# Two Fourier stages by sums and differences on quarter arrays, and operations recorded when they are counted ready

## The chip, the core and the metric

The kernel runs on one core of one Trainium2 chip. The metric is the device time of one execution in microseconds (us). TensorE (PE) multiplies matrices into PSUM, VectorE (DVE) and ScalarE (ACT) read and write PSUM and SBUF, GpSimd (POOL) works in SBUF and issues indirect DMAs, and SyncE (SP) issues the other DMAs. Each engine works through its own queue in order. PSUM is used as seven banks of 128x512 numbers and one more for logits.

## The reference

`x` has 8 batches of 2496 rows with 256 channels. Along the rows a filter is applied in the frequency domain, and every row of the result then goes through one of eight experts:

```python
X = np.fft.rfft(x, axis=1)
y = np.fft.irfft(X * (filt_r + 1j * filt_i), n=2496, axis=1)
x = y.reshape(19968, 256)
logits = x @ w_gate                          # 8 experts
expert_idx = np.argmax(logits, axis=1)
gate_w = softmax(logits)[row, expert_idx]
out[row] = gate_w * (np.maximum(x[row] @ w1[e], 0) @ w2[e])   # w1 256x1024, w2 1024x256
```

All numbers are float32.

## The kernel before

A Fourier transform of 2496 = 39 x 64 rows is done in two steps, of 39 points (index q) and of 64 points (index t). Each batch goes through four stages. `stage_a` (line 498) multiplies by the table `tas`, which has the cosines and sines of 39 points three times along its diagonal: 3 values of t lie in 3 x 39 = 117 partitions, and 3 x 40 rows come out, 20 cosine and 20 sine rows for each. 22 such columns of 256 channels make a batch, and they come in chunks of four, `CH`, the last of two. A matmul takes two columns, 512 numbers a partition. The result goes through the DRAM tensor `zd` to change its layout. `stage_b` (511) does the 64 points and multiplies by the filter, `stage_c` (533) goes back over 64 points and writes `ud`, and `stage_d` (548) goes back over the 39 points with the table `tds`. Batch 0 goes through SBUF instead of DRAM (`first_a`, `turn_z`, `first_c`, `turn_u`). From `stage_d`'s rows the logits are made (`turn_y` with `logits`, or from batch 3 on `block_logits`), `route` (707) finds each row's expert and its place in a sorted list, and `scatter` writes the rows to the DRAM tensor `rowsd` by an indirect DMA. `tile_map` plans expert tiles of 512 rows (256 and 128 at the start and the end).

The experts' work: `rows_in` loads a tile, `turn_x` (954) transposes it in blocks on DVE, `hidden_by_quarters` (979) forms the hidden layer by seven products of quarter matrices with sums of weights (`w1_sums`) and rows (`sums`) from POOL, and `result` (1042) multiplies by the second weights, scales by the gate and writes the output by an indirect DMA.

The order is worked out while the program is built. `Order` (125) wraps the engines: each call goes to the real engine at once and is counted with an estimated duration, so that it has a clock for every engine and a ready time for every tile. The main loop (from 1287) picks PE's next step: the steps of the Fourier stages stand in the list `STEPS` (made by `slot`, 1071, one slot for each batch), the products of the experts in two streams, and `share` decides how much of each. A step is taken when what it needs is counted ready. `either` (373) gives an evacuation of PSUM to DVE or to ACT, whichever is counted to end first. What a step makes other engines do is recorded at that place, and so stands in their queues in PE's order:

```python
def issue(*args, **named):
    self.order.count(self.name, op, args, named)
    return real(*args, **named)
```

`flush` and `more_loads` record the stores and loads on SP's queue, `prefetch` the loads of rows and weights, `side` a piece of `route`. All calls are recorded in the line 238, so the profile tells operations apart by their tiles: `fin` is a loaded chunk of any stage, `zo`, `uo` and `yo` are what stages one, three and four write, `hT` the hidden layer, `xg` and `xT` an expert tile's rows before and after transposition, `w1t` and `w2t` weights.

Of the kernel before, what the change touches and what calls it, by code (L numbers as in the profile page):

```python
# [34 lines left out]
TK = NB * NS  # L35
DH = D // P
# [4 lines left out]
NJ = D // CT  # L41

# [13 lines left out]
def dft_tables():  # L56
# [25 lines left out]
    ids = np.zeros((NB, N1, NG))  # L82
    valid = np.zeros((NB, N1, NG))
    for j in range(NB):
        for i in range(len(range(j, N2, NB))):
            ids[j, :, i] = token(q, NB * i + j)
            valid[j, :, i] = 1.0

    by_block = np.zeros((4, CT, NG + 2))
    by_block.reshape(P, NG + 2)[:TP, :NG] = valid.reshape(TP, NG)  # L90
# [5 lines left out]
        "ta": ta.reshape(TP, TK),  # L96
        "tb": tb,
        "tc": tc,
        "td": np.pad(td.reshape(TK, TP), ((0, 0), (0, P - TP))),
        "sg": np.concatenate([sg[:, :NF // 2], sg[:, NF // 2:]]),  # L100
        "ids": ids.reshape(TP, NG),
        "valid": np.concatenate([np.pad(valid.reshape(TP, NG), ((0, P - TP), (0, 0))), by_block], axis=1),
    }


def lay_x(x):

    out = np.zeros((x.shape[0], P, NG, D), x.dtype)
    q = np.arange(N1)
    for j in range(NB):  # L110
        for i in range(len(range(j, N2, NB))):
            out[:, j * N1:(j + 1) * N1, i] = x[:, token(q, NB * i + j)]
    return out
# [11 lines left out]
class Order:  # L125
# [3 lines left out]
    LOAD = 2.0  # L129

    def __init__(self, nc):
        self.nc = nc
        self.t = dict.fromkeys(("tensor", "vector", "scalar", "gpsimd", "sync", "transfers"), 0.0)
        self.slow = self.busy = self.last = 0.0
        self.done, self.used, self.slots, self.ahead = {}, {}, {}, {}
        self.tensor, self.vector, self.scalar, self.gpsimd, self.sync = (
            Issue(self, name) for name in ("tensor", "vector", "scalar", "gpsimd", "sync"))
# [6 lines left out]

    def ready(self, *aps):
        times = [a for a in aps if isinstance(a, float)]
        return max([0.0] + times + [self.done.get(key, 0.0) for a in aps if not isinstance(a, float) for key in self.parts(a)])
# [29 lines left out]
    def count(self, engine, op, args, named):  # L177
        aps = [a for a in list(args) + list(named.values()) if isinstance(a, bass.AP)]
        if not aps:
            return  # L180
# [6 lines left out]
        at = named.get("out_offset")  # L187
        if at is not None:
            ins.append(at.ap)
        kept = [a for a in ins if a.space != DRAM or a.name[:2] in ("zd", "ud")]  # L190
        free = self.t[engine]
        start = max([free] + [self.ready(a) + (self.HOP if engine != "sync" else 0.0) for a in kept])
        if out is not None:
            start = max(start, self.ahead.pop(out.name, 0.0))
            n = int(np.prod([d[1] for d in out.ap][1:])) if out.space != DRAM else 0
        tail = 0.0
        if op.endswith("dma_start"):
            busy = 1.3 if engine == "gpsimd" else 0.4
            self.t[engine] = start + busy
            took = self.transfer(out, named["in_"])  # L200
            self.t["transfers"] = max(self.t["transfers"], start + busy) + took
            end, tail = self.t["transfers"], self.LOAD
        else:
            if out is None:
                took = 0.02
            elif engine == "tensor":
                if start > self.busy + 1.2:
                    self.slow = start + 3.4
                rows = out.ap[0][1]
                took = max(0.1, 0.00085 * n) if op == "transpose" else max(0.216, 0.00169 * n) if rows > 32 else 0.00045 * n  # L210
                took *= 2.0 if start < self.slow else 1.0
                tail = 0.25
            elif engine == "vector":
                took = 0.15 + n / 960
            elif engine == "scalar":
                took = 0.16 + n / 1200
            else:
                took = 0.2 + n / 480
            end = self.t[engine] = start + took
            if engine == "tensor":  # L220
                self.busy = end
# [4 lines left out]
        self.last = end + tail  # L226


class Issue:
# [3 lines left out]
    def __getattr__(self, op):  # L233
        real = getattr(getattr(self.order.nc, self.name), op)

        def issue(*args, **named):
            self.order.count(self.name, op, args, named)
            return real(*args, **named)  # L238

        return issue  # L240


class Slots:
    def __init__(self, order, pool, bufs):
        self.order, self.pool, self.bufs, self.tiles, self.n = order, pool, bufs, {}, {}

    def free(self, tag, k=0):

        past, n = self.tiles.get(tag, []), self.n.get(tag, 0)
        if len(past) + k < n or k >= n:  # L250
            return 0.0
        name = past[k - n]
        return max(self.order.done.get(name, 0.0), self.order.used.get(name, 0.0)) + 0.1

    def tile(self, shape, dtype, **named):
        new = self.pool.tile(shape, dtype, **named)
        past = self.tiles.setdefault(named.get("tag") or named.get("name"), [])
        n = self.n[named.get("tag") or named.get("name")] = named.get("bufs") or self.bufs
        if len(past) >= n:
            name = past[-n]  # L260
            self.order.ahead[new.name] = max(self.order.done.get(name, 0.0), self.order.used.get(name, 0.0)) + 0.1
        past.append(new.name)
        return new


@with_exitstack
def kernel(
# [39 lines left out]
    TR = E * TE  # L307

# [16 lines left out]
    prow = perm.tile([P, 1], I32, name="prow")  # L325
    need = perm.tile([1, 1], I32, name="need")
    ps = open_pool(ctx, name="ps", bufs=7, space=PSUM)

# [4 lines left out]

    tas = cst.tile([TP, TK], F32, name="tas")
    tbs = cst.tile([P, P], F32, name="tbs")
    tcs = cst.tile([P, P], F32, name="tcs")
    tds = cst.tile([TK, P], F32, name="tds")
# [15 lines left out]
    ids0 = cst.tile([TP, NG], F32, name="ids0")  # L353
    vld = cst.tile([P, 2 * NG + 2], F32, name="vld")
# [8 lines left out]
    def experts_pool():  # L363
        first.close()
# [8 lines left out]
    def either(i, n, on_vector, on_scalar):  # L373

        ready = nc.ready(i)
        if max(t["vector"], ready) + 0.15 + n / 960 <= max(t["scalar"], ready) + 0.16 + n / 1200:
            on_vector()
        else:
            on_scalar()

    def evac(o, i, n):
        either(i, n, lambda: nc.vector.tensor_copy(o, i), lambda: nc.scalar.copy(out=o, in_=i))
# [8 lines left out]
    def load_filters(c):  # L391
        f0, n = FH[c]
        if c == 0:
            nc.sync.dma_start(out=tbs, in_=tb)
# [11 lines left out]
        if c == 0:  # L406
            nc.sync.dma_start(out=tcs, in_=tcm)

    def load_rest():
        nc.sync.dma_start(out=tds, in_=td)  # L410
# [33 lines left out]
    def columns(ap, i0, n):  # L444
# [3 lines left out]
        yield TK, slice(0, m), rows[i0 * TK:(i0 + m) * TK, :].rearrange("(i p) d -> p i d", p=TK)  # L448
        if m < n:
            yield NS, slice(m, n), rows[(NG - 1) * TK:, :].rearrange("(i p) d -> p i d", p=NS)  # L450

    ins, outs, lgs, yts, lands = {}, {}, {}, {}, []
    NIN, YB = 7, 6
# [17 lines left out]
    def by_part(ap):  # L471

        return ap.rearrange("t (c f) d -> (t c) f d", c=2)

# [8 lines left out]
    def load_z(b, c):  # L483
        f0, n = FH[c]
        zi = fin(("z", b, c))
        nc.sync.dma_start(out=zi[:, :n], in_=by_part(zd[b])[:, f0:f0 + n, :])

    def load_u(b, c):
        i0, n = CH[c]
        ui = fin(("u", b, c))  # L490
        for r, m, v in columns(ud[b], i0, n):
            if r == TK:

                v = bass.AP(v.tensor, v.offset, [[D, P]] + [list(k) for k in v.ap[1:]])
                r = P
            nc.sync.dma_start(out=ui[:r, m], in_=v)

    def stage_a(b, c):
        i0, n = CH[c]
        xt = ins.pop(("x", b, c))  # L500
        zo = sb.tile([TK, 4, D], F32, tag="st", name="zo", bufs=4)
        for j in range(0, n, 2):
            p = bank()
            mm(p[:TK, :], lhsT=tas, rhs=xt[:TP, j:j + 2, :], start=True, stop=True)
            evac(zo[:, j:j + 2, :], p[:TK, :].rearrange("p (t d) -> p t d", t=2), 512)
        for r, m, v in columns(zd[b], i0, n):
            move(v, zo[:r, m])
# [3 lines left out]
    def stage_b(b, f):  # L511
# [6 lines left out]
        mm(p, lhsT=tbs, rhs=zi[:, j:j + 2, :], start=True, stop=True)  # L518
# [9 lines left out]
        if b == 0 or b < 3 and not sides:  # L528
            nc.gpsimd.tensor_tensor(ys, ys, yw, op=ALU.add)
        else:  # L530
            nc.vector.tensor_tensor(ys, ys, yw, op=ALU.add)

    def stage_c(b, f):
# [6 lines left out]
        mm(p, lhsT=tcs, rhs=ys, start=True, stop=True)  # L540
        evac(uo[:, j:j + 2, :], p.rearrange("p (i d) -> p i d", i=2), 512)
        if j == 2:
            f0 = f - 2
            move(by_part(ud[b])[:, f0:f0 + 4, :], uo)
# [3 lines left out]
    def stage_d(b, c):  # L548
# [8 lines left out]
        for j in range(0, n, 2):  # L557
            p = bank()
            if i0 + j + 2 < NG:
                mm(p, lhsT=tds, rhs=ui[:TK, j:j + 2, :], start=True, stop=True)  # L560
            else:

                for i, k in enumerate((TK, NS)):
                    mm(p[:, i * D:(i + 1) * D], lhsT=tds[:k, :], rhs=ui[:k, j + i, :], start=True, stop=True)
            evac(yo[:, j:j + 2, :D], p.rearrange("p (i d) -> p i d", i=2), 512)

# [824 lines left out]
```

## Time and profile before

| | before |
|---|---|
| median of 3 runs (lowest, highest) | 1497.58 us (1494.55, 1498.59) |
| profiled execution | 1494.36 us |
| its span, first to last instruction | 1492.7 us |
| mean granted clock of PE in it | 0.991 |
| PE, DVE, ACT, POOL busy | 1451.7, 770.7, 471.8, 733.4 us |
| memory read and written | 196.45 and 80.64 MB |

In a group's line the names are what is written <- what is read, then partitions x numbers; of a matmul the rows*columns of the array in use come first. Behind x stands how many there were, then their busy time together, the mean duration of one, the engine's idle time before them, and what ended it. PEld is the loading of weights into the array, beside PE. A float32 product is two records of PE.

### The profile page before, as it was taken

The numbers are of one execution on the slowest core, as the hardware profiler recorded it, in microseconds if no ns is written. First come the engines' busy times: TensorE is split into PE (matmuls) and PEld (weight loads), VectorE is DVE, ScalarE is ACT, GpSimd is POOL, SyncE is SP. The second block draws the span as 40 slices with busy tenths as digits, with TensorE's granted clock in tenths as the row PEclk, the third lists the DMA queues.
The fourth block names the chain that finished last, engine by engine and source line by source line (L and its number), as shares of the span: only waits on it lengthen the run. The fifth ranks groups of instructions, "written<-read, shape, count | busy, mean of one in ns | idle before, by whom it ended". The sixth has DMA issues, their size and how long they took to land. (4 is left out here: it accounts for less than half of the span.)

```text
span 1492.7 us, 24448 instructions
## 1 busy us (share of the span) xinstructions
PE 1451.7 (97%) x7396; PEld 1148.8 (77%) x7396; DVE 770.7 (52%) x1732; ACT 471.8 (32%) x983; POOL 733.4 (49%) x1053
## 2 busy tenths in 40 slices
PE   8898997999989999999999999999999999999998
PEld 6553555776667777777787888887888889999997
DVE  4667677354577656565764555537344334441110
ACT  4453442333322233222233222222222222223332
POOL 3434455344446656554555756764546455741111
PEclk9999999999999999999999999999999999999999
DMA  9749889678767756474456545545455543456661
GB/s 255 252 152 333 289 306 295 207 258 280 251 182 229 219 157 169 131 239 128 128 152 196 130 117 149 147 139 145 151 178 176 167 146 106 117 187 179 181 179 52
DMA packets 216376, 278.10 MB, mean 186 GB/s; under 512 B 124131, under 2 KB 163708, under 8 KB 216245
## 3 DMA queue, kind: packets, MB, share of 16 engines
q1 hardware_dynamic: 197125, 233.19, 52.7%
q0 software_dynamic: 19120, 43.33, 8.3%
q8 instruction: 62, 1.02, 0.3%
q14 instruction: 69, 0.57, 0.1%
HBM read 196.45 MB, written 80.64 MB: 186 GB/s over the span
## 5 line engine op out<-in xcount | busy, mean ns | idle before, releaser
L238 DVE TENSOR_TENSOR hT<-bank,hT 128x512 f32<-128x512 f32 (+1 forms) x504 | 300.7, 627 | 298.9 <-PE bank L238 183.1
L238 PE MATMUL bank<-w2t,hT 128*128 128x256 f32 x1984 | 447.5, 382 | 1.0 <-DVE hT L238 0.5
L238 PEld LDWEIGHTS bank<-w2t,hT 128*128 128x128 f32 x1984 | 377.6, 191 | 62.9 <-issue 9.5
L238 POOL DMA_INDIRECT out_dram<-ys,ng x161 | 160.7, 998 | 459.7 <-ACT ys L238 183.3
L238 PE MATMUL bank<-xT,w1t 128*128 128x256 f32 (+1 forms) x1728 | 316.7, 329 | 0.3 <-DVE xT L238 0.3
L238 PEld LDWEIGHTS bank<-xT,w1t 128*128 128x128 f32 x1728 | 266.8, 192 | 36.5 <-issue 11.8
L238 ACT ACTIVATE hT<-hT 128x1024 f32<-128x1024 f32 (+1 forms) x144 | 133.9, 958 | 378.7 <-DVE hT L238 374.8
L238 POOL DMA_INDIRECT rows<-yo,row x176 | 180.3, 1025 | 69.0 <-POOL yo L238 36.0
L238 ACT ACTIVATE ys<-bank,ng 128x256 f32<-128x256 f32 x128 | 60.6, 473 | 369.6 <-PE bank L238 297.0
L238 PE MATMUL bank<-sums,wsum 128*128 128x256 f32 (+1 forms) x576 | 135.7, 358 | 2.8 <-DVE hT L238 1.8
L238 PE MATMUL bank<-w2s,hT 128*128 x592 | 132.6, 380 | 0.0
L238 PEld LDWEIGHTS bank<-w2s,hT 128*128 128x128 f32 x592 | 110.5, 191 | 13.6
L238 PEld LDWEIGHTS bank<-sums,wsum 128*128 128x128 f32 x576 | 101.2, 191 | 20.1 <-issue 7.3
L238 DVE TENSOR_TENSOR ys<-bank,ht 128x512 f32<-128x512 f32 x80 | 55.0, 688 | 81.9 <-PE bank L238 77.3
L238 PE MATMUL bank<-fin,tas 117*120 117x512 f32 x154 | 76.9, 620 | 11.9 <-DMA fin<-in_x_dram 11.9
L238 PE MATMUL bank<-fin,tds 120*128 120x512 f32 (+1 forms) x168 | 76.6, 576 | 6.0 <-DMA fin<-ud 6.0
L238 DVE STREAM_TRANSPOSE xT<-xg 128x512 f32<-128x512 f32 (+2 forms) x126 | 57.5, 494 | 44.2 <-PE bank L238 44.2
L238 PE MATMUL bank<-fin,tbs 128*128 128x512 f32 x140 | 72.6, 605 | 2.5 <-DMA fin<-zd 2.5
L238 ACT ACTIVATE hT<-bank 128x128 f32<-128x128 f32 (+1 forms) x192 | 58.1, 304 | 50.1 <-PE bank L238 42.4
L238 PE MATMUL bank<-ys,tcs 128*128 128x512 f32 x140 | 72.7, 604 | 1.0 <-DVE ys L238 1.0
L238 POOL TENSOR_TENSOR wsum<-w1t 128x256 f32<-128x256 f32 x72 | 53.4, 742 | 38.1 <-PE bank L238 36.5
L238 PE MATMUL bank<-xT,wsum 128*128 128x256 f32 (+1 forms) x288 | 68.3, 360 | 0.3 <-DVE hT L238 0.3
(150 smaller groups left out, 1491.5 us busy)
## 6 DMA issues: line engine op xcount, KB each, us to landing
w1t<-in_moe_w_dram SPq DMA_DIRECT2D x126, 512.0 KB
w2t<-in_moe_w_dram SPq DMA_DIRECT2D x68, 512.0 KB
fin<-in_x_dram SPq DMA_DIRECT2D x39, 512.0 KB
fin<-zd SPq DMA_DIRECT2D x35, 512.0 KB
ud<-uo SPq DMA_DIRECT2D x35, 512.0 KB
fin<-ud SPq DMA_DIRECT2D x35, 512.0 KB
zd<-zo SPq DMA_DIRECT2D x35, 480.0 KB
xg<-rows SPq DMA_DIRECT2D x112, 128.0 KB
```

The source lines that it names most:

```text
L238: return real(*args, **named)
```

## The change

Three things change together.

First, in batches 3 to 7 (`BQ = 3`) stages one and four use that the cosine of q and of 39 - q is the same and the sine the opposite. The rows are laid out so that q and 39 - q stand in the same partition, in columns two apart; `fold_x` replaces a loaded chunk by sum and difference, cosines are taken of the sums and sines of the differences, from 60 partitions each, and the four products of a chunk (cosine or sine, first or second 64 partitions) each use a quarter of the array. Stage four does the reverse, `fold_y` makes rows q and 39 - q from the two parts. Batches 0 to 2 keep their stage one; their stage four and their routing go by the new layout of rows, in which 124 partitions are used where there were 117 and unused places are sent to an index past the end of the list, which the scatter drops. Each table has a second version, loaded when the last batch of the first is through.

Second, calls to DVE, ACT and POOL are held (`Held`) and recorded when their start is counted to be no later than PE's clock, in the order of these starts; operations that can run on either of two engines choose only then. A matmul or DMA that needs a held one's result has it recorded first. PE's steps count a tile that a held operation writes as not ready.

Third, smaller edits: PSUM banks and load buffers are taken in the order in which they come free; `turn_x` transposes in place (`xg`, three buffers, read in runs of 32) where it wrote `xT`; the hidden layer is in halves, and `result` takes them in the order in which they are finished; weights and rows are asked for only when a buffer is counted free within 0.5 us; the addition at the end of `stage_b` is given to DVE or POOL by counted time; a tiny memset stands between two row scatters that follow each other on POOL.

```diff
 class Order:
+    def given(self, engine, op, args, named):
+        if self.caught is not None:
+            self.caught.append((engine, op, args, named))
+            return None
+        if engine in self.HELD and self.hold:
+            self.held.append(Held(self, [(engine, op, args, named)]))
+            return None
+        out, ins = self.operands(op, args, named)
+        self.clear([key for a in ins for key in self.parts(a)], self.parts(out) if out is not None else [])
...
+    def advance(self):
+        while True:
+            free = [(work.begin(), k) for k, work in enumerate(self.held) if not work.behind]
+            begin, k = min(free, default=(self.NEVER, 0))
+            if begin > self.t["tensor"]:
+                return
+            self.held[k].go()
...
+    def issue(self, engine, op, args, named):
+        if engine == "gpsimd":
+            row = op == "indirect_dma_start" and named["out"].name[:4] == "rows"
+            if row and self.rows_last:
+                self.nc.gpsimd.memset(self.between, 0.0)
...
+class Held:
+    def go(self):
+        while self.behind:
+            next(iter(sorted(self.behind, key=self.order.held.index))).go()
...
+        made = order.issue(*min(self.ways, key=end))
...
     def evac(o, i, n):
-        either(i, n, lambda: nc.vector.tensor_copy(o, i), lambda: nc.scalar.copy(out=o, in_=i))
+        nc.one_of(lambda: nc.vector.tensor_copy(o, i), lambda: nc.scalar.copy(out=o, in_=i))
...
-    NIN, YB = 7, 6
+    NIN, YB, OB = 7, 6, 1
...
+    def fold_x(b, c):
+        m = CH[c][1] // 2
+        xt = ins["x", b, c]
+        od = outs["od", b, c] = sb.tile([P, 2, D], F32, tag="od", name="od", bufs=OB)[:, :m]
+        sums(od, xt[:, :m], xt[:, m:2 * m], ALU.subtract)
+        sums(xt[:, :m], xt[:, :m], xt[:, m:2 * m], ALU.add)
...
     def stage_a(b, c):
-        for j in range(0, n, 2):
-            p = bank()
-            mm(p[:TK, :], lhsT=tas, rhs=xt[:TP, j:j + 2, :], start=True, stop=True)
-            evac(zo[:, j:j + 2, :], p[:TK, :].rearrange("p (t d) -> p t d", t=2), 512)
...
+            od = outs.pop(("od", b, c))
+            both = [bank()[:, :m * D].rearrange("p (t d) -> p t d", t=m) for _ in range(2)]
+            for c2, of in enumerate((xt, od)):
+                for h in range(2):
+                    k = slice(64 * h, 64 * h + TH)
+                    mm(both[h][64 * c2:64 * c2 + 64], lhsT=ta[k, 64 * c2:64 * c2 + 64], rhs=of[k, :m], start=True, stop=True)
+            for h in range(2):
+                evac(zo[:, h * m:(h + 1) * m, :], both[h], m * D)
...
     def stage_d(b, c):
+        for h in range(2):
+            last = i0 + n == NG and h == 1
+            for k in range(2):
+                if b < BQ:
+                    rows, cols = slice(0, NS if last else TK), slice(64 * k, 64 * k + 64)
+                else:
+                    rows, cols = slice(64 * k, 64 * k + (NF if last else TH)), slice(0, 64)
+                mm(both[k][64 * h:64 * h + 64], lhsT=tds[rows, cols], rhs=ui[rows, h * m:(h + 1) * m, :], start=True, stop=True)
...
+    def sums(o, i0, i1, op):
+        nc.one_of(*(lambda on=on: on.tensor_tensor(o, i0, i1, op=op) for on in (nc.vector, nc.gpsimd)))
+
+    def fold_y(b, c):
+        m = CH[c][1] // 2
+        yo, odd = outs["o", b, c], outs.pop(("odd", b, c))
+        sums(yo[:, m:2 * m, :D], yo[:, :m, :D], odd, ALU.subtract)
+        sums(yo[:, :m, :D], yo[:, :m, :D], odd, ALU.add)
...
     def turn_x(i):
-        xts[i] = pools["moe"].tile([P, DH, 4 * P], F32, tag="xT", name="xT", bufs=2)
-        for dh in range(DH):
-            nc.vector.transpose(xts[i][:, dh, :n * P].rearrange("p (g r) -> p g r", r=QW), xg[:, :n * NQ, dh, :])
+        xg = xg[:, :n * NQ]
+        nc.vector.transpose(xg, xg)
+        xts[i] = xg.rearrange("p g h r -> p h g r")
...
     def result(i, j):
-        for k in range(FT):
+        for m, k in enumerate((0, 1, 4, 5, 6, 7, 2, 3)):
...
     def slot(k):
+        for name, of, at, when in (("ta", ta, BQ - 1, "a"), ("tb", tb, BQ, "b"), ("tc", tcm, BQ, "c"), ("td", td, BQ + 1, "d")):
+            if k == at:
+                steps.append((-1.0, lambda name=name, of=of: load_table(name, of, 1), None, 0.0, when))
...
+                    steps.append((at - 0.04, lambda c=c: fold_x(k + 1, c), ("x", k + 1, c), 0.0, "x", lambda c=c: count("od") < OB and [ins["x", k + 1, c]]))
...
     def prefetch():
-        if i < min(len(work), NT - RARE) and rows_at[work[i][3]] <= t["tensor"] and i - used["x"] < 2:
+        if i < min(len(work), NT - RARE) and rows_at.get(work[i][3], nc.NEVER) <= t["tensor"] and i - used["x"] < 2 and i - halves[0] // 2 < 3 and soon("xg"):
...
             flush()
             more_loads()
+            nc.advance()
```

## The prediction

> **What bounds the kernel now.** I read the page from the top: busy time by engine first, then what TensorE (PE) waits for, then the timeline and the groups of the two stages that change.
>
> ```profile
> span 1492.7 us, 24448 instructions
> PE 1451.7 (97%) x7396; PEld 1148.8 (77%) x7396; DVE 770.7 (52%) x1732; ACT 471.8 (32%) x983; POOL 733.4 (49%) x1053
> PEclk9999999999999999999999999999999999999999
> DMA  9749889678767756474456545545455543456661
> ```
>
> PE is the bound: 41.0 us of the span without a matmul, and every other engine is idle for about half. DMA is near full only in the first quarter. So a matmul taken away shortens the span wherever PE has other products to go on with. The list of PE's waits says what the idle time is:
>
> ```profile
> PE bank L238 <- DMA fin<-in_x_dram: 12.3, 6, 6.9
> PE bank L238 <- DMA fin<-ud: 6.0, 1, 6.0
> PE bank L238 <- DVE hT L238: 3.6, 4, 1.8
> PE lt L238 <- DVE yt L238: 3.1, 1, 3.1
> PE bank L238 <- DMA fin<-zd: 2.5, 2, 2.3
> ```
>
> The columns are total, times, longest. Loads end 20.8 us (three lines), other engines some 14 us (two of these lines and eight smaller ones). All of it lies before 1050 us, nearly all before 450 us (the other 6 us of the 41 are the span's end). The groups, by form, give the stages that change:
>
> ```profile
> L238 PE MATMUL bank<-fin,tas 117*120 117x512 f32 x154 | 76.9, 620 | 11.9 <-DMA fin<-in_x_dram 11.9
> L238 PE MATMUL bank<-fin,tds 120*128 120x512 f32 x140 | 68.0, 610 | 6.0 <-DMA fin<-ud 6.0
> ```
>
> 154 records stand for the 77 products of batches 1 to 7 with 11 each, so a product is two passes. The 620 ns overlap the next pass; what one costs is the distance between starts, from the timeline:
>
> ```profile
> 637.24 1.88 PE L238 MATMUL bank<-fin,tbs 128*128 128x512 f32 x4
> 638.95 1.89 PE L238 MATMUL bank<-xT,w1t 128*128 128x256 f32 x8
> ...
> 303.67 2.11 PE L238 MATMUL bank<-w2t,hT 128*128 128x256 f32 x9
> 305.70 0.65 PE L238 MATMUL lt<-yt,wb 128*32 128x128 f32 x16
> 306.28 1.13 PE L238 MATMUL bank<-xT,w1t 128*128 128x256 f32 x4
> ```
>
> From 637.24 to 638.95 four passes of 512 columns take 1.71 us: 0.43 each (0.216 for 256 columns, by the eight passes to 640.68). The lower lines are the nearest to the new form: 16 passes of 128 columns, each in a strip of 32 columns of the array. One after the other they would take 16 x 0.11 = 1.76; they take 305.70 to 306.28, 0.58 us. So four strips run side by side, four rounds of 0.11. Changing to strips and back costs the rest: nine passes of 0.216 after 303.67 end at 305.61, 0.09 before the strips start, and 0.58 - 0.44 = 0.14 behind them: 0.23 us in and out.
>
> **The change part by part.**
>
> Stage one, batches 3 to 7. Before: 5 x 11 products of two passes at 0.43 = 47.2 us. After, by the order of the built program: 25 groups of four 64x64 products of 512 columns and 5 of 256. If all four run side by side a group is two passes, 0.86 or 0.43: 23.6. Gain 23.6.
>
> Stage four, batches 3 to 7. Before: 5 x 10 products at 0.86, and the last pair of columns in 5 x 4 passes of 256 at 0.27 to 0.31 (distance of starts), 1.16 a batch: 48.7. After: 25 x 0.86, and 5 x 0.86 for the last one, whose 60-row and 20-row parts follow each other: 25.7. Gain 23.0. Together 46.6.
>
> Changes of tiling. The order shows 263 changes of the array's form after, 127 before: 136 more, 68 in-and-out pairs at 0.23: +15.6. Strips of 32 columns are the nearest row; quarters of 64x64 have no row. Ends: 0.09 x 136 = 12.2, and twice the pair, 31.
>
> Stage four, batches 0 to 2, also changes: 120x64 products, the two of the lower output half before the two of the upper, on the same strip. Beside each other they cost what two full products did; if the second pair comes up only when the first pair's last pass starts, a group takes three rounds of two passes' time where two were: +0.86 on 15 groups, +13 at most. The trace shows one waiting pass being overtaken by other strips, not three; I take +5, ends 0 and +13. Nine mask multiplications more on DVE (237 ns each) are 2 us off the path. Transposes of batches 0 to 2 are 124 wide where 117 were: 132 x 7 columns, +1.
>
> Folds. fold_x and fold_y add 120 additions (100 of 128x512, 20 of 128x256), 71 on DVE and 49 on POOL by their place in the built order. A DVE addition of two SBUF tiles takes 732 ns (ys<-ys,yw), on POOL 1270 ns. That is about +50 us on DVE and +57 on POOL, less 10 ys additions that go from POOL to DVE: both stay under 56% of the span. It lies beside expert products, which run from about 160 us on, when batch 3 starts. I cost it at nothing on PE; without that cover a group waits for one pair, 1.5 us on DVE or 2.5 on POOL, and 60 groups for 90 us. Engine queues: DVE and POOL have behind the folds the hT additions and the wsum sums that PE needs; since folds are given out when counted ready, what queues behind one is late by 0.7 to 1.3 us.
>
> Queues. SP issues 74 more DMAs (stores of z and loads of u in two halves, second tables), at 0.33 to 0.45 us an issue in SP's timeline: +30 us over 700 us, on a queue that waits 450 us for PE. The loads of the second tables wait for the last reader of the first; PE meets them with other products. Uncovered, four waits like the 6.0 us of fin<-ud: 24. POOL gets 16 tiny memsets, about 3 us. turn_x in place is one transposition of 128x1024 (1235 ns at yt<-yo) where two of 686 stood: 4 us off DVE, off the path. Reading it in runs of 32 is what the strips of yt above do at 0.11 a pass: free.
>
> Held operations. They change no PE instruction's cost, only who waits. Idle POOL waits 183.3 us in out_dram for ys on ACT, and ACT 374.8 us in hT for DVE, with other work behind them; given out when ready these no longer block it, and SP asks for weights only when a buffer is about to be free. What can go is PE's 34.8 us of named waits, plus the slow clock behind them (0.991 granted: 13.4 us): at most 48. Against it, a wrong count makes PE wait in a fixed order. Ends -48 and +42 (rival two). I take half of the 14 us that engines end and a third of the 20.8 that loads end: -14, next late being the loads of the first 250 us, which are DMA-bound.
>
> Sum: 1492.7 - 46.6 + 15.6 + 5 + 1 - 14 = 1453.7. The profiled execution took 1494.36, 1.7 more than its span; the median of the runs is 3.2 above that: 1458.6.
>
> **Two rules against the change.** The 16 passes above, two for each of eight products, took 0.58 us, four rounds of 0.11 and the way back. [...]
>
> The second: ACT's copy out of a bank of 512 columns takes 586 ns (zo<-bank) and DVE's 684. [...] Two copies on ACT are 1.17 against a group's 0.86; were all 50 full groups held for the difference, +16 us. I take nothing: expert products stand between the groups and seven banks are there.
>
> **Rivals.**
>
> One, the row halves take turns. Strips of columns are shown side by side, halves of rows nowhere. Then a group takes 1.72 again, the 46.6 are lost and the costs stay: 1505. It decides from 1.5 us a group on (46.6 - 7.6 net costs, over 60, is 0.65 above 0.86). For it: no row. Against: four strips need four streams, two halves two.
>
> Two, slower: PE waits at stage one for the folds. od has one buffer, so the second fold starts only after the first group's products; if each of the 30 groups waits for one pair on DVE, 1.4 us, +42, and the order's gain of 14 does not come: 1515. It decides when PE's idle time, 41 us now and some 27 in the forecast, goes above 65. For it: the order is fixed, and the counted times differ from the traced ones (POOL's addition is counted 1.27, DVE's 0.68 against 0.73). Against: DVE is idle half of the time and the loads are asked for seven buffers ahead.
>
> Three, the order removes most waits: -40 in place of -14: 1432. For it: the idle time sits in a few places (6.9, 6.0, 3.1 us). Against: the largest are loads.
>
> **How the numbers follow.** Forecast, 1440 to 1478, 0.58; three 0.16; two 0.13; one 0.07; 0.06 for products side by side with waits that eat most of the gain, near 1490. The range leaves out 2 in 10: it reaches to 1422, ten below rival three, and to 1502, where the unknown costs at their ends (+15 tiling, +8 stage four, +22 waits) meet rival one. Within 0.3% (4.5 us), which is what this kernel's runs can tell, lies 0.04 (the upper end of the last case and the lower of rival one); faster is 0.58, 0.16 and 0.05 of the last case, 0.79; the rest, 0.17, is slower.
>
> **What would show it.** Right: fin,ta and od,ta start in fours within some 30 ns, two rounds a group; PE busy near 1427; PE's waits on od, fin by DVE or POOL absent; the chain of work still ending in the expert products' scatter. Wrong: starts of the two row halves 0.43 us apart (rival one); PE waiting on DVE or POOL for fin, od or yo (rival two); changes of form above 0.3 us in and out; new waits for fin in the first 300 us.

## The result, and the profile after

The changed kernel takes 1513.7 us, median of four runs (1512.7 to 1516.2), against 1496.1 for the kernel before beside it: a ratio of 1.0121, with the interval 1.0096 to 1.0146. The forecast was 1458.6 with a range up to 1502: wrong in its sign and outside its range. The profiled execution took 1513.4 us, 2.1 more than its span.

The first lines of the page of the kernel after: span, busy time by engine, granted clock and DMA in 40 slices.

```profile
span 1511.3 us, 25589 instructions
PE 1449.1 (96%) x7718; PEld 1116.3 (74%) x7718; DVE 830.2 (55%) x1700; ACT 491.0 (32%) x1052; POOL 846.7 (56%) x1108
PEclk9999999999999999999999999999999999999999
DMA  9759877867987766676447345655556343455661
```

PE is still the bound. Its busy time fell by only 2.6 us (1451.7 to 1449.1), where some 25 was forecast, and its idle time rose from 41.0 to 62.2. POOL's busy time rose by 113 us; the folds were to add 57.

What PE waits for in the kernel after (total, times, longest):

```profile
PE bank L306 <- POOL fin L306: 20.5, 8, 8.6
PE bank L306 <- DVE hT L306: 5.4, 4, 2.5
PE bank L306 <- POOL ys L306: 5.1, 2, 3.7
PE bank L306 <- DMA fin<-in_x_dram: 4.9, 2, 2.9
PE bank L306 <- DVE ys L306: 3.9, 3, 1.6
```

Before, loads led this list and POOL had one line of 1.0 us. Now POOL leads: `fin` is what fold_x writes. The loads of stage one went from 12.3 to 4.9 us, as hoped, and POOL took their place. All waits in PE's list together went from 34.8 us to 55.6. The mean granted clock went from 0.991 to 0.982; at the longest wait, shown below, the trace has it at 0.50 from 219.9 to 226.7 us, and at 1.00 before and behind.

What the changed products cost shows in the distances between starts. For each kind of group I take the median distance, in the trace's matmul records, from its first start to the start of the next matmul, changes of the array's form included, times the number of such groups in the program (us):

| products | before, one group | all | after, one group | all |
|---|---|---|---|---|
| stage one, batches 3 to 7: 25 full groups, 5 last ones | 1.72, 0.86 | 47.3 | 1.02, 0.59 | 28.5 |
| stage four, batches 3 to 7: 25 and 5 | 1.72, 1.15 | 48.8 | 1.02, 1.16 | 31.3 |
| stage four, batches 0 to 2: 15 and 3 | 1.72, 1.15 | 29.3 | 1.88, 2.01 | 34.2 |

Together that is 125.3 before and 94.0 after, 31 us less; the prediction's terms for them (-46.6, +15.6 and +5) make -26. So the products did what was forecast and somewhat more. The span is 18.6 us longer all the same, so all the rest, the waits (20.8 us more in the list) and the lower clock (0.982 for 0.991, at most some 14 us) above all, took some 49 us more, where 14 less was forecast.

PE's timeline in the kernel after (start, duration, what) shows the products themselves:

```profile
208.28 0.65 PE L306 MATMUL bank<-fin,ta 60*64 60x512 f32 x2
208.29 0.65 PE L306 MATMUL bank<-od,ta 60*64 60x512 f32 x2
208.76 0.60 PE L306 MATMUL bank<-fin,ta 60*64 60x512 f32 x2
208.77 0.60 PE L306 MATMUL bank<-od,ta 60*64 60x512 f32 x2
209.30 1.94 PE L306 MATMUL bank<-fin,td 120*64 120x512 f32 x8
211.17 1.06 PE L306 MATMUL bank<-ident,yo 124*128 124x124 f32 x8
```

Four passes, one of each 64x64 product, start within 20 ns, and the four second passes 0.48 us later. A group takes 1.02 us from start to start with its changes of form; two full products took 1.72. The eight 120x64 passes of stage four of batches 0 to 2 take 1.87 with a change of form, which is the 1.72 of four passes of 0.43 and little else. Their records start in four pairs, the two of a pair 13 ns apart. One behind the other, eight passes at the 0.43 of the full products would take 3.44, so I take a pair for one pass in each strip, although in the program's order three more passes of the first strip stand ahead of the other strip's first.

Now the price on POOL that the prediction does not have. All scatters of rows, one line of each kernel's answer for that tile (durations in ns, least/median/most; then the first and last start). Before:

```profile
L238 POOL DMA_INDIRECT rows<-yo,row x176: 913/1002/1567, 91.3 to 994.1; - x176
```

After:

```profile
L306 POOL DMA_INDIRECT rows<-yo,row x176: 1321/1338/1862, 94.6 to 947.5; - x176
L306 POOL DMA_INDIRECT rows<-fill,pad x8: 972/988/992, 1141.0 to 1180.6; - x8
```

The same 176 scatters take 0.34 us more each. Their indices and rows have 124 partitions now, where 168 of them had 117 (and the last of each batch 39); the eight scatters of padding rows, with 128, still take 0.99. That is 242.5 us of POOL against 180.3 in all, between 95 and 950 us, where the folds lie too. POOL's timeline shows one place where it reaches PE (the bracket is the idle time before, and what ended it):

```profile
211.34 0.99 POOL L306 DMA_INDIRECT out_dram<-ys,ng  x1 [1.28 <-DMA out_dram<-ys,ng]
212.32 0.35 POOL L306 COPY yo<-rs 124x8 f32<-124x8 f32 x2
212.85 1.35 POOL L306 DMA_INDIRECT rows<-yo,row  x1 [0.19 <-POOL yo L306]
214.21 0.09 POOL L303 MEMSET between<- 1x8 f32 x1
214.51 1.32 POOL L306 DMA_INDIRECT rows<-yo,row  x1 [0.20 <-issue]
...
218.18 1.33 POOL L306 DMA_INDIRECT rows<-yo,row  x1 [0.30 <-DMA fin<-ud]
219.52 0.19 POOL L306 COPY yo<-rs 124x8 f32<-124x8 f32 x1
222.09 1.26 POOL L306 TENSOR_TENSOR fin<-fin 128x512 f32<-128x512 f32 x1 [2.38 <-issue]
```

DVE in the same stretch:

```profile
209.51 0.69 DVE L306 COPY zo<-bank 128x512 f32<-128x512 f32 x1 [1.31 <-DMA fin<-in_x_dram]
220.06 0.69 DVE L306 COPY yo<-bank 128x512 f32<-128x512 f32 x1 [9.86 <-DMA rows<-yo,row]
...
221.26 0.68 DVE L306 TENSOR_TENSOR od<-fin 128x512 f32<-128x512 f32 x1
```

And PE:

```profile
223.40 1.12 PE L306 MATMUL bank<-fin,ta 60*64 60x512 f32 x2 [8.59 <-POOL fin L306]
```

POOL works through a row of scatters. The buffer `yo` is free only when its scatters are done, so a copy into it stands 9.86 us at the head of DVE's queue; behind it, in an order that is fixed when the program is built, stands the subtraction that makes `od`. Only then may POOL write the sum into `fin`, over the subtraction's input, and PE, whose queue has that product next, is idle for 8.59 us and starts at a granted clock of 0.50 (1.12 us a pass where 0.65 stands above).

### The profile page after: what moved, and what is told of

It is laid out like the page before. It is cut to its first block, busy times and chain, and to the rows that moved or that the text cites. A ratio compares the mean times of both kernels' runs of the same rounds, so it can differ in the third digit from the quotient of the medians.

```text
span 1511.3 us, 25589 instructions
## 1 busy us (share of the span) xinstructions
PE 1449.1 (96%) x7718; PEld 1116.3 (74%) x7718; DVE 830.2 (55%) x1700; ACT 491.0 (32%) x1052; POOL 846.7 (56%) x1108
## 3 DMA queue, kind: packets, MB, share of 16 engines
q0 software_dynamic: 33456, 43.58, 9.9%
## 5 line engine op out<-in xcount | busy, mean ns | idle before, releaser
L306 PE MATMUL bank<-xg,w1t 128*128 128x256 f32 (+1 forms) x1728 | 318.3, 330 | 1.3 <-ACT uo L306 1.3
L306 PEld LDWEIGHTS bank<-xg,w1t 128*128 128x128 f32 x1728 | 266.5, 192 | 39.8 <-issue 8.2
L306 POOL DMA_INDIRECT rows<-yo,row x176 | 242.5, 1378 | 65.0 <-POOL yo L306 36.9
L306 ACT ACTIVATE ys<-bank,ng 128x256 f32<-128x256 f32 x159 | 75.4, 474 | 420.8 <-PE bank L306 341.2
L306 DVE STREAM_TRANSPOSE xg<-xg 128x1024 f32<-128x1024 f32 (+2 forms) x63 | 53.6, 851 | 131.3 <-DMA xg<-rows 94.5
L306 PE MATMUL bank<-ys,tc 128*128 128x512 f32 x140 | 79.5, 654 | 11.3 <-POOL ys L306 5.1
L306 PE MATMUL bank<-fin,ta 60*64 60x512 f32 (+2 forms) x164 | 56.1, 637 | 23.5 <-POOL fin L306 20.5
L306 PE MATMUL bank<-fin,tb 128*128 128x512 f32 x140 | 73.8, 614 | 1.8 <-DVE hT L306 1.8
L306 PE MATMUL bank<-sums,w1t 128*128 128x256 f32 (+1 forms) x288 | 67.5, 357 | 3.0 <-DVE hT L306 3.0
L306 PE MATMUL bank<-xg,wsum 128*128 128x256 f32 (+1 forms) x288 | 68.2, 359 | 0.0
```

What stands on the lines that cost most here:

```text
L306: return getattr(getattr(self.nc, engine), op)(*args, **named)
```

## The experiments

Times are medians; ratios are against the kernel before, run on the same chip beside each. Differences between two versions are of medians, though some of them ran on different chips.

**Theory one: the held order itself is what fails.** Holding is turned off; folds and products stay.

```diff
-        self.held, self.hold, self.caught = [], True, None
+        self.held, self.hold, self.caught = [], False, None
```

> The changed kernel with holding switched off: calls to DVE, ACT and POOL are recorded at once, in PE's order, as before; the quarter products, the new row layout and the smaller edits stay. If the held order makes PE wait (theory one), the gain of the products comes back: 1455 to 1475 us, PE's idle time back to some 40 us. If the folds themselves make PE wait (theory two: one od buffer, a fold pair behind POOL's row scatters), it stays at 1505 or goes above, with PE waiting for fin, od or yo. If the slower row scatters (theory three: 1378 ns in place of 1025, 176 of them, 62 us of POOL) are what delays all, it stays near 1510 with POOL named before PE's waits.

Measured: 1590.7 us, 1.0641 [1.061, 1.0671]. Holding is worth 77 us to this kernel, and theory one falls.

**The folds alone taken back.** All batches take the form without folds, holding stays on.

```diff
-BQ = 3
+BQ = 8
```

> The changed kernel with BQ = 8: no batch uses sums and differences, stage one is as before and stage four by 120x64 products in all batches; holding stays. Theory one: slower than the kernel before by what holding costs, 1520 to 1540 us. Theory two: no fold, so no wait for one: 1480 to 1500, at or under the kernel before. Theory three: 1505 to 1520, as the 176 scatters of 124 rows stay.

Measured: 1533.9, 1.0257 [1.0212, 1.0302]. With holding on, the folds with their products are worth 20 us, so they are not what lost the time either.

**Both taken back** (both edits above): what is left are the new layout of rows, its scatters and the small edits.

> BQ = 8 and holding off together: what is left of the change are the new row layout, its scatters of 124 rows with a bound, and the smaller edits. Theories one and two: near the kernel before, 1490 to 1505 us. Theory three: 1510 and more, with row scatters at 1.35 us.

Measured: 1562.8, 1.046 [1.0428, 1.0493]. With both named parts of the change out, the kernel is 68 us slower than before, so a loss sits in what came along with them. Holding gains with the folds and without (77 and 29 us). The folds gain only with it: without holding they cost 28 (1562.8 to 1590.7).

**The scatters.** Those of batches 3 to 7 send all 128 partitions of the tile, the unused ones with an index past the list's bound, where the changed kernel cuts them at 124. Nothing else moves: the planner counts both alike, and in the two traces PE, DVE, ACT and POOL each have the same instructions in the same order.

```diff
-            rows.append((row[:YR, i:i + 1], yos[i // 4][:YR, i % 4, :]))
+            rows.append((row[:R, i:i + 1], yos[i // 4][:R, i % 4, :]))
```

> The changed kernel, in which the row scatters of batches 3 to 7 send 128 partitions in place of 124 (the four more have an index past the end and are dropped). If the count of 124 is what made the scatter 1.34 us, these 110 go back to about 1.0 us and POOL is busy 37 us less; theory three then expects 1490 to 1500 us, the other two 1505 to 1515. If the bound or the dropped rows are the cause, they stay at 1.34 us.

Measured: 1497.6, 1.0016 [0.9998, 1.0035]. Sixteen us come back from four partitions more per scatter, with the order unchanged. All scatters of this kernel, 110 of 176 of them wider now:

```profile
L306 POOL DMA_INDIRECT rows<-yo,row x176: 967/1004/1834, 92.3 to 928.7; - x176
```

**All 176 at 128 partitions** (R = P for batches 0 to 2 as well, their logits' tile cleared first):

```diff
-        R, mask = YR, vld[:YR, t0:t0 + w]
+        R, mask = P, vld[:, t0:t0 + w]
...
+                nc.gpsimd.memset(lgs[b], 0.0)
```

> All 176 row scatters send 128 partitions in place of 124 (batches 0 to 2 too; a logits tile is cleared first). In the run with 110 of them at 128 these went from 1.34 to 1.00 us and the time from 1513.7 to 1497.6. If slow scatters hold up the yo buffers, and so DVE's queue in PE's busiest stretch with transfers (160 to 300 us), the other 66 bring as much again: 1483 to 1492, under the kernel before, with PE's wait for fin on POOL below 10 us. If what is left of the loss lies elsewhere (folds, edits), 1495 to 1499.

Measured: 1487.1, 0.9948 [0.9928, 0.9968]: faster than before. Together with the 16 above the scatter's width is worth 26.6 us of the changed kernel. The last 10.5 of them are less sure than the 16: here the planner's order changed as well. The first lines of PE's waits in it:

```profile
PE bank L306 <- issue: 8.0, 5, 3.2
PE bank L306 <- DVE ys L306: 7.1, 6, 1.9
PE bank L306 <- DVE hT L306: 6.0, 4, 2.2
```

`fin` by POOL, 20.5 us above, is no longer in the list.

**Was it the planner's count, rather than the time?** The planner counts 1.3 us for POOL's indirect DMAs; here 1.65, so that it knows of the 1.34 and the 0.30 us of idle time that follow each other in POOL's timeline.

```diff
-            return 1.3 if engine == "gpsimd" else 0.4
+            return 1.65 if engine == "gpsimd" else 0.4
```

> The changed kernel with its 124-partition scatters, but the planner counts an indirect DMA on POOL at 1.65 us where it counted 1.3 (the trace has 1.34 and 0.30 idle before it, where the kernel before had 1.00 and 0.30). Nothing on the chip gets faster; only the order changes. If the held order suffers because its count of POOL runs 0.35 us ahead at each scatter, most of what 128 partitions bring comes back without them: 1495 to 1503. If POOL's time itself is the loss, it stays at 1508 to 1518.

Measured: 1550.9, 1.0376 [1.0354, 1.0398], 37 us worse than the changed kernel and outside both expected ranges; PE then waits 18.5 us for `yo` on ACT and 11.4 for `yt` on DVE. The count became truer for the 176 row scatters and falser for the 161 scatters of the output, which take 1.01 us and are counted 1.65 too. So whether a true count of the row scatters alone would have helped stays open. What the run does show is how much the order alone can move: with no instruction made slower, the time rose by 37 us. Of the other edits only that of the 110 scatters leaves the order alone; the rest change it too, and none of them separates that from what the edit is meant to change.

**The rest of the change with good scatters:** all 176 at 128 partitions, without folds and without holding.

> No folds (BQ = 8), no holding, all scatters at 128 partitions. Without the last point this was 1562.8. If the slow scatter was most of the 67 us that this version lost against the kernel before, 1500 to 1515; if the smaller edits lose it (stage four in two banks by 120x64 products, transposition in place, loads asked for late), 1535 to 1550.

Measured: 1513.0, 1.0119 [1.0097, 1.0141]. So 50 of the 68 us of that kernel were the scatters; 17 are the rest. Most of these 17 have a name: without folds stage four goes by 120x64 products in all eight batches, and its 40 full groups take 1.87 us where 1.72 stood, its 8 last ones 2.01 where 1.15 stood, together some 13 us.

**The fourth corner:** scatters at 128, holding on, no folds.

> All row scatters at 128 partitions, holding on, stages one and four of all batches in the form without folds (the fourth corner: with folds it took 1487.1, without folds and without holding 1513.0). The prediction's terms give 14 for the order that holding makes and, from -46.6 for the products, 12.6 measured for form changes and 8 of form changes that this kernel has too, some 40 less on TensorE for the folds: 1513 - 14 = 1499 for this kernel if the order's term was right, and the folds would then be worth 12 only because their waits took the rest. Rival: holding is worth more without the folds (29 us where the scatters had 124 partitions): 1484, and the folds are then worth nothing or cost 3. Third: holding is worth nothing here: 1513, and the folds 26.

Measured: 1503.3, 1.007 [1.0044, 1.0096]. The corners, in us:

| | 124 partitions | 128 partitions |
|---|---|---|
| neither | 1562.8 | 1513.0 |
| holding alone | 1533.9 | 1503.3 |
| folds alone | 1590.7 | not run |
| both | 1513.7 | 1487.1 |

With good scatters holding is worth 9.7 us without the folds (some 7 by the ratios, which allow for the chip) and the folds 16.2 with holding. By the medians of the groups the folds take stages one and four of batches 3 to 7 from 104.1 us (47.3, and 25 groups of 1.87 with 5 of 2.01) to 59.8: 44 us less, of which 28 are lost again elsewhere. PE's listed waits go from 22.4 us to 38.9 between the two kernels, those on DVE among them from 5.0 to 24.3.

**The folds on VectorE alone,** and the additions of ys too, with all scatters at 128:

```diff
-        nc.one_of(*(lambda on=on: on.tensor_tensor(o, i0, i1, op=op) for on in (nc.vector, nc.gpsimd)))
+        nc.vector.tensor_tensor(o, i0, i1, op=op)
```

> All scatters at 128 partitions, and the 120 fold additions and the ys additions always on DVE in place of the engine counted to end first. If folds that stand behind scatters in POOL's queue make PE wait (POOL fin 20.5 us, POOL ys 5.1 us in the changed kernel), another 15 to 25 us less than with all scatters at 128: 1465 to 1475. If DVE is then the late one, the same as that run or up to 15 us more.

Measured: 1482.4, 0.9911 [0.9892, 0.993]: 4.7 us less, where 15 to 25 were expected, and hardly clear of the noise, since the two intervals overlap. What PE waits for then is mostly loads:

```profile
PE bank L306 <- DMA w2t<-in_moe_w_dram: 7.1, 2, 6.2
PE bank L306 <- DMA fin<-in_x_dram: 4.2, 2, 2.8
PE bank L306 <- DMA w1t<-in_moe_w_dram: 4.1, 1, 4.1
PE bank L306 <- DMA fin<-zd: 3.8, 1, 3.8
```

**A second buffer for each of od and odd,** at the cost of one of the seven for loaded tiles:

```diff
-    NIN, YB, OB = 7, 6, 1
+    NIN, YB, OB = 6, 6, 2
```

> The best kernel so far (all scatters at 128, folds on VectorE: 1482.4), with two buffers each for the differences od and odd in place of one, and six in place of seven for the tiles read in stages one, two and four to make the room. If the one buffer of od and odd is what keeps folds and products late (a fold must wait until the product before has read its difference), the waits before products of stages one and four fall from some 17 us by my count of start-to-start time and the time to 1470 to 1478. If late loads are what is left (19 us of TensorE's waits end with a load), six buffers for loaded tiles make it worse: 1485 to 1500.

Measured: 1471.5, 0.9847 [0.9828, 0.9866], 10.9 us better in spite of the buffer given up, and the best version: 1.5% faster than the kernel before. All lines of loads together fell from 21.4 us to 12.3:

```profile
PE bank L306 <- DMA fin<-in_x_dram: 6.6, 3, 4.8
PE lt L306 <- DVE yt L306: 5.2, 3, 3.0
PE bank L306 <- DVE ys L306: 4.3, 3, 1.9
PE bank L306 <- DMA fin<-ud: 3.2, 2, 1.8
```

So most of what had looked like late loads of weights (11.2 us in the list above, 0.8 now) went away with the one buffer, or with the order that changed with it.

**The seventh buffer back, and a sixth `yo` given up:**

```diff
-    NIN, YB, OB = 6, 6, 2
+    NIN, YB, OB = 7, 5, 2
```

> As the best kernel (all scatters at 128, folds on VectorE, two buffers each for od and odd: 1471.5), but with seven buffers for loaded tiles again and the room taken from the finished rows yo, five in place of six. If late loads for stages one, two and four are what is left of TensorE's waits there (fin from in_x 6.6, ud 3.2, zd 1.7: 11.5 us), the seventh buffer lets them go earlier and the time is 1460 to 1468. Rival: loads are late because SyncE's queue stands behind other waits, not for want of a buffer, and a yo that is held until its scatters are done is then the scarcer: 1472 to 1485, with yo back among TensorE's or VectorE's waits.

Measured: 1482.1, 0.9918 [0.9896, 0.9941]. The rival was right on the time: the sixth `yo` is worth more than the seventh loaded tile. Its sign shows in part: the waits of ACT and DVE for a `yo` whose scatters are not done rise from 6.2 us to 15.9. Of PE's own waits `yo` ends only 1.3 us, and `ys` on DVE leads them with 10.7. The diff is against the version above.

**The price of a scatter by its partitions, alone.** 16 more scatters, one for each count, from one tile of zeros to rows of their own behind the list's end, none with an index past the bound:

```diff
+            for k in range(2 * e, 2 * e + 2):
+                m = (64, 96, 112, 113, 116, 117, 118, 119, 120, 121, 122, 123, 124, 125, 126, 127)[k]
+                scatter("pad", more[:m, k:k + 1], fill[:m], top=TR + 16 * P)
```

> The kernel with every row scatter at 128 partitions (1487 us), and beside its 8 scatters of padding rows 16 more to rows of their own behind the end of the list, one each with 64, 96, 112, 113, 116 to 127 partitions, all with the same bound and from the same tile, none with an index over the bound. So only the number of partitions differs. Theory one (the count itself sets the price, by how it is cut into packets): the one with 124 takes about 1.34 us, the one with 117 about 1.00, and other counts fall on one of a few such steps. Rival (the price of 124 came from rows over the bound that fall away, or from the routing's own data): 124 takes about 1.0 here too, as 117 and 120 do. The program's time is 1487 plus what 16 to 20 us of scatters on POOL add near the end: 1487 to 1505; it tells nothing else.

The end of the series in POOL's timeline: the scatters from `more` have 122, 123, 124, 125, 126 and 127 partitions, those from `pad` 128.

```profile
1154.81 1.70 POOL L306 DMA_INDIRECT rows<-fill,more  x1 [0.23 <-issue]
...
1156.82 1.42 POOL L306 DMA_INDIRECT rows<-fill,more  x1 [0.23 <-issue]
...
1159.84 0.98 POOL L306 DMA_INDIRECT rows<-fill,pad  x1 [0.30 <-issue]
...
1161.14 1.36 POOL L306 DMA_INDIRECT rows<-fill,more  x1 [0.23 <-issue]
...
1162.80 1.21 POOL L306 DMA_INDIRECT rows<-fill,more  x1 [0.21 <-issue]
...
1167.02 1.01 POOL L306 DMA_INDIRECT rows<-fill,more  x1 [0.23 <-issue]
...
1168.35 2.58 POOL L306 DMA_INDIRECT rows<-fill,more  x1 [0.23 <-issue]
```

124 takes 1.36 us with nothing over the bound and no routing behind it: theory one holds in that, the rival falls. But the prices are not a few steps. The program took 1498.6 us in its one run, within what was expected.

## Why the prediction was wrong

**The failed step is one that it does not have.** The prediction followed the width of the transposes from 117 to 124 and priced it at +1, and passed over the same 117 to 124 in the 176 row scatters on POOL. They went from 1.00 to 1.34 us. No row of the trace of before would have priced it, since it has scatters of 117 and of 128 partitions only, both near 1.0, and the last one of each batch with 39, at 0.92; but the count changed, and that deserved a bound. With POOL's row scatters the largest group on that engine, a few tenths on each is 60 us on POOL; it is worth 26.6 us of the changed kernel's time, 16.1 of them shown with the order of every engine unchanged.

**"I cost it at nothing on PE", of the folds, failed too,** for the reason that rival two gave and the prediction set aside. Its cover, the expert products, was there; the queue order was not. With good scatters the folds gave 16.2 us, when their products' own gain was 44. Putting them on VectorE came with 4.7 less and a second buffer for od and odd with 10.9: if that last gain is the buffer's, "od has one buffer" was the right sentence, in the wrong part of the text. Rival two's price, 1515, is close to the 1513.7 measured, and PE's idle time of 62.2 us is just under the 65 from which it was to decide; but half of its work was done by the scatters, which it doesn't name, so the agreement is luck.

**The terms for the products were right.** A full group of four takes two passes' time, 0.86, and 0.16 for the change of form in and out, where 0.23 was taken. For stage four of batches 0 to 2 the +5 is what came out, 4.9, but not as it was thought: a full group costs little more than its change of form (1.88 for 1.72), and half of the sum lies in the three last groups (2.01 for 1.15), which the prediction did not count. In batches 3 to 7 the last groups of stage four take 1.16 for the 0.86 assumed, no less than before. Rival one, row halves by turns, falls by the four starts within 20 ns. Nor do `od`'s products wait for the second passes of `fin`'s: `od`'s first ones start at 208.29 us, `fin`'s second ones at 208.76. That the copies out of the banks (two on ACT take 1.17 us, a group was set at 0.86) would hold the groups hardly shows: PE's waits that end with an ACT instruction, its copies out of banks among them, are 3.8 us in all after the change, where the prediction's estimate for all 50 full groups was +16; taking nothing was nearly right.

**The order's -14 was right in sign.** With good scatters and no folds it measured -9.7, and PE's listed waits there are 22.4 us against 34.8 before the change. With slow scatters it was worth 29 us, and 77 with the folds; that such an order gains most where another engine blocks fits these numbers but was not tried by itself.

**Queues.** For 74 more DMAs on SP the prediction set an end of 24 us if uncovered: PE's waits that end with a load sank from 20.8 us to 11.1 in the changed kernel (4.9, 3.2 and 3.0), so the cover held. The 16 memsets are 0.09 us each, 1.5 in all, where about 3 was assumed.

**The sum,** from 1458.6 forecast to 1513.7: 26.6 for the scatters' width, 4.7 with the folds off POOL, 10.9 with second buffers, each the difference of one edit on the version before it; 12.9 are left. Only 16.1 of the 26.6 are free of a change of order, and 4.7 is within the noise. Some 4 of the 12.9 may be holding's -9.7 against -14. The others lie with the folds as far as is known: the best version is 31.8 us faster than the one with holding and no folds (1503.3 to 1471.5), where the products alone got 44 cheaper. Which waits make that, `fin` from in_x (6.6), `yt` (5.2) and `ys` (4.3) being the longest in its list, and whether another order would spare them, stays open. The small edits were not undone one by one; beside the 13 us of stage four's form they leave only some 4 of the 17 us without folds and holding.

## What to carry to other kernels

When a change alters the number of partitions of a tile, go through every instruction that takes the tile, the indirect DMAs first, and choose a count that took little here (117, 120, 126 and 128 took 0.98 to 1.03 us, 124 took 1.36 and 127 2.58) or simply send all 128 with the surplus indices out of bounds: four unused partitions more in 110 of the scatters were worth 16 us, and in all 176 of them 27. Before costing work at nothing because it lies beside other work, ask what stands ahead of it in its engine's queue and how many buffers let it go early: with a second buffer the same folds came out 11 us better. When an order is worked out by counted times, compare an edit's gain with what another order alone can do, here 37 us, before calling the cause shown. When a change of several parts loses, run the corner with all named parts out: here it was slower by 68 us, which told at once that the cause had no name yet.

## What the runs showed of the hardware that was not expected

The time for which an indirect scatter kept POOL, 0.94 to 2.58 us, went in these runs with how its number of partitions divides. The 16 scatters of one run, with the largest divisor up to 16, and the number of partitions divided by it:

| partitions | largest divisor to 16 | quotient | us |
|---|---|---|---|
| 64, 96, 112 | 16 | 4, 6, 7 | 0.94, 0.95, 0.95 |
| 120 | 15 | 8 | 1.03 |
| 126 | 14 | 9 | 1.01 |
| 117 | 13 | 9 | 1.01 |
| 121 | 11 | 11 | 1.03 |
| 119 | 7 | 17 | 1.10 |
| 125 | 5 | 25 | 1.21 |
| 116 | 4 | 29 | 1.28 |
| 124 | 4 | 31 | 1.36 |
| 123 | 3 | 41 | 1.42 |
| 118, 122 | 2 | 59, 61 | 1.65, 1.70 |
| 113, 127 | 1 | 113, 127 | 2.38, 2.58 |

A line through the first and the last, 0.94 + 0.0133 x (quotient - 4), meets all the others to within 0.06 us. The limit of 16 is assumed; the run shows only that 17 must not count as a divisor: 119, 17 times 7, takes 1.10 us, where 112 with the quotient 7 takes 0.95. There is one scatter of each count, so it is a fit to this run; 117 before (1.00, 168 scatters), 124 after (1.34, 176) and 128 with all at 128 (0.98, 176) agree, each by its median, and so do the eight of 39 before, 13 by 3, with 0.92. It shows in the packets as well: the software queue moved 19120 before, 33456 after and 16560 with all scatters at 128, for the same 43.3 to 43.6 MB, which is 96 packets less for each of the 176 when four partitions are added.

Why the price goes with this division, no run shows.

In the trace of the kernel after, passes of 120x64 products overtook more than one waiting pass, if a pair of starts is one pass in each strip: three wait in one strip, and the other strip's passes start beside it all the same (four pairs, 13 ns apart within a pair, 1.87 us for all eight).
